# Scoring VectorE's block ahead of the single block in an attention kernel on Trainium2

## The chip, the cores and the metric

The kernel runs on one NeuronCore of a Trainium2 chip. The metric is the device time of one execution in microseconds. TensorE (PE) multiplies matrices, ScalarE (ACT) evaluates functions such as the exponential, VectorE (DVE) and GpSimd (POOL) do elementwise work, and SyncE (SP) issues transfers. Each engine works through its own instruction list in order; semaphores tie the lists together.

## The reference

Two transformer layers of self-attention and a feed-forward part, on 2048 rows of 512 numbers in bfloat16, 32 heads of 16:

```python
def _A_ref(x, wqkv, wo):
    H = 32; Dh = D // H
    q, k, v = split(x @ wqkv)                 # by head
    scores = jnp.einsum("bhqd,bhkd->bhqk", q, k) * Dh ** -0.5
    p = softmax(scores, axis=-1)
    o = jnp.einsum("bhqk,bhkd->bhqd", p, v)
    return merge(o) @ wo

def _B_ref(x, w1, w2):                        # w1: 512 x 1792
    return silu(x @ w1) @ w2

x = A_x
x = x + _A_ref(_layernorm(x), A_wqkv, A_wo)
x = x + _B_ref(_layernorm(x), B_w1, B_w2)
x = x + _A_ref(_layernorm(x), A_wqkv, A_wo)
x = x + _B_ref(_layernorm(x), B_w1, B_w2)
return x
```

`split` and `merge` stand for the reshapes and transposes by head.

## The kernel before

**Blocks and steps.** The attention scores are cut into blocks: one head, 128 keys (one k tile, `kt`), 512 queries. Four heads that lie on four strips of 32 partitions (`j` = 0 to 3) make a group of four blocks; a step handles one group. The steps are one long list, over both layers, the query chunks `qc`, the head groups `g`, two parities `par` and the 16 k tiles: 1024 of them after the opening. In each step `score` issues one matmul per block, with 32 contraction rows, so that the four of a step sit on different row strips of TensorE's array.

**Who makes the exponentials.** Nearly every step has four blocks in three kinds of home:
- the *pair*: two blocks in a two-bank PSUM tile (tag `s2`, two such tiles in turn), for one ScalarE exponential over 1024 numbers per partition;
- the *single block*: one bank (tag `s1`, one buffer), for a ScalarE exponential over 512;
- *VectorE's block*, d: one bank (tag `sd`, one buffer, tile `d_ps`). `emit_d` scores it and VectorE turns it into the bits of a half-precision approximation of the exponential with one `tensor_scalar` into `d_y` (L1001). It belongs to the group that is four steps ahead. Whenever two d blocks are done, GpSimd makes two more terms from them (`d_z`, L1021).

Steps 5 to 12 have no d block of their own and two single blocks (`n1 == 2`, the second one in the bank `sd`). ScalarE does the exponential of the single block first, then that of the pair (both L1083). Every second step, `emit_pv` issues the products of the probabilities with the values (L876).

**The order of TensorE's list.** A loop in Python writes every engine's list by hand (`manual_schedule`), step by step: the pair, the single block, d, then copies of finished sums, the products with the values if it is their turn, the exponentials, and last background work. All engines are in order: a matmul that waits for its bank holds up all matmuls behind it.

**The planner.** Background work (projections, layer norm, the feed-forward part, the closing of finished head groups) is written as generators that give way at each `part(...)` with its price. `Model` keeps a clock for TensorE (`pe`), ScalarE (`act`) and VectorE (`dve`), and the times at which banks come free: `s1`, `s2`, `sd`. `Model.scores` and `Model.score_d` move these on for a step's scores. `Background.heads` offers the next pieces, and `Model.fits` admits one if it ends before ScalarE would run out of work, and if what it needs has landed by the clock of its engine:

```python
if landed > (self.pe if pe else self.dve):
    return False
```

Three of these background pieces are named later. `group_out` closes a head group: after a DMA transpose of its sums into `ot` it takes a reciprocal (L601, priced 0.25) and multiplies (L603, priced 0.43) into `attn`. `ffn` computes one tile of the hidden layer with four matmuls into a bank with one buffer (`h_ps`, L466), in two halves of two matmuls; ScalarE takes a tanh of it (L649), and VectorE's `silu_mul` (L652) then reads the bank for the last time. `ln_apply` (L402) normalises rows and sends them through a DMA transpose. Where a step has no background matmuls and no products, `fill` adds matmuls with zero weights if the planner sees room.

Of the kernel before, what the change touches and what calls it, by code (L numbers as in the profile page):

```python
# [109 lines left out]
class Model:  # L110
# [26 lines left out]
            self.pe += self.SWITCH  # L137
            self.mode = mode

    def scores(self, a, d):  # L140
        self.to("S")
        self.pe = max(self.pe, self.s2[0], self.s1, self.sd if a == 4 else 0.0)
        self.scored = self.pe + self.GROUP + self.TO_ACT
        if d and a == 3:
            self.score_d()
        self.pe += self.GROUP

# [71 lines left out]
def kernel(  # L219
# [13 lines left out]
    S, D = xf.shape  # L233
# [96 lines left out]
    for par in range(2):  # L330
        m = const.tile([P, 1], FP32, name=f"mask{par}")
# [517 lines left out]
    def score(blk, out):  # L849
        L, qc, pi, g, par, kt, j = blk  # L850
        r = slice(32 * j, 32 * j + 32)
        nc.tensor.matmul(  # L852
            out,
            lhsT=KT[L, kt // 4][r, g, (kt % 4) * P : (kt % 4 + 1) * P],
            rhs=QT[g][r, par, :],
            start=True,
            stop=True,
        )
# [134 lines left out]
    def emit_d(t, blk):  # L993

        s_ps = psum["s"].tile([P, 512], FP32, name="d_ps", tag="sd", bufs=1)
        score(blk, s_ps[:])
        if not pairs or len(pairs[-1]["ds"]) == 2:
            y = dpool.tile([P, 2, 512], U16, name="d_y", tag="y", bufs=Y_BUFS)
            pairs.append(dict(ds=[], y=y))
        pr = pairs[-1]  # L1000
        nc.vector.tensor_scalar(  # L1001
            out=pr["y"][:, len(pr["ds"]), :],
            in0=s_ps[:],
            scalar1=float(1024 * SCALE * math.log2(math.e)),
            scalar2=float(1024 * (15 - SHIFT)),
            op0=ALU.mult,
            op1=ALU.add,
        )
        d = dict(blk=blk, pair=len(pairs), left=NT)
        d["rhs"] = [(t + 1, 0, pr["y"][:, len(pr["ds"]), :].bitcast(FP16))]  # L1010
        pr["ds"].append(d)
        d_todo.append(d)
        if len(pr["ds"]) == 2 or blk == last_d:
            other_terms(t, pr)
# [31 lines left out]
    with tc.manual_schedule(  # L1046
        engines={ENG.PE, ENG.Activation, ENG.DVE, ENG.Pool, ENG.SP}
    ):
        with psum_whole("a"):
            w_ps = bank("warm")  # L1050
            for i in range(56):
                nc.tensor.matmul(w_ps[:, 0:P], lhsT=ident[:], rhs=ident[:], start=True, stop=True)
            new_v(0, 0)
            xnT[0, 0] = xslot(0, "xnT")
            ln = [run(ln_stats(0, (i, i + 1))) for i in (0, 2)]
            for i in (0, 2):
                mv, rstd = ln[i // 2]
                xns = [ln_apply(0, i + u, mv[:, u, :], rstd[:, u, :]) for u in range(2)]
                ln_transpose(i, xns, xnT[0, 0], nc.vector.tensor_copy if i else nc.scalar.copy)
            bg.done["ln", 0, 0] = 0.0  # L1060
            bg.add(("k", 0, 0, 0), proj_k(0, 0, 0))
            bg.add(("q", 0, 0, 0, 0), proj_q(0, 0, 0))
            bg.ensure(("q", 0, 0, 0, 0))
        stream_psum = ExitStack()
        stream_psum.enter_context(psum_stream())
        for g in range(1, NG):
            bg.add(("k", 0, 0, g), proj_k(0, 0, g))
            bg.add(("q", 0, 0, g, 0), proj_q(0, 0, g))
            if g == 1:
                bg.add(("v", 0, 0), proj_v(0, 0))  # L1070
        for c in range(1, NC):
            bg.add_side(None, ln_ahead(c))
            bg.add_side(("ln", 0, c), ln_attn(0, c))
            bg.add(("k", 0, c, 0), proj_k(0, c, 0))
            bg.add(("v", 0, c), proj_v(0, c))
            for g in range(1, NG):
                bg.add(("k", 0, c, g), proj_k(0, c, g))

        m = Model(DVE_SLACK, PE_MARGIN)
        bg.model = m  # L1080

        def exp(p_sb, s_ps):
            nc.scalar.activation(  # L1083
                p_sb,
                s_ps,
                ACT.Exp,
                bias=-SHIFT * math.log(2.0) + math.log(EXP_SUM),
                scale=float(SCALE),
            )

        def flat(x):
            return x.rearrange("p a b -> p (a b)")

        def score_pair():
            return psum["s"].tile([P, 2, 512], FP32, name="s_ps", tag="s2", bufs=2)

        p_pre = hpool.tile([P, FT, 512], BF16, name="p_pre", tag="hT")
        pre = [score_pair() for _ in range(2)]
        for j in range(4):
            score(steps[0][0][j], pre[j // 2][:, j % 2, :])  # L1100
        for i in range(2):
            exp(flat(p_pre[:, 2 * i : 2 * i + 2, :]), flat(pre[i][:]))
        p_tiles[0] = [p_pre[:, i, :] for i in range(4)]
        m.act = 2 * m.EXP2
        m.s2 = [m.EXP2, m.act]

        early[0] = m.early = True
        bg.ensure(("q", 0, 0, 1, 0))
        for t in range(1, len(steps)):
            a_blks, d_blks = steps[t]  # L1110
            for L, qc, pi, g, par, kt, j in a_blks + d_blks:
                bg.ensure(q_of[L, qc, pi, g, par])
                if qc == 0:
                    bg.ensure(("k", L, kt // 4, g))
            L, qc, pi, g, par, kt, j = a_blks[0]
            if kt == kts_of[L, qc, pi, g, par][0]:
                for Lq, c, gq, n in q_next.get((L, qc, pi, g, par), []):
                    bg.add(("q", Lq, c, gq, n), proj_q(Lq, c, gq), first=True)
            s2 = score_pair()[:]
            n1 = len(a_blks) - 2  # L1120
            s1 = [
                psum["s"].tile([P, 512], FP32, name="s1_ps", tag=tag, bufs=1)[:]
                for tag in ("s1", "sd")[0:n1]
            ]
            for i in range(2):
                score(a_blks[n1 + i], s2[:, i, :])
            for i in range(n1):
                score(a_blks[i], s1[i])
            if n1 == 1:
                for blk in d_blks:  # L1130
                    emit_d(t, blk)
            m.scores(len(a_blks), len(d_blks))
            while after:
                after.pop()()
                m.sums()
            if t in pv_steps:
                m.pv(emit_pv(t, pv_step(t)))
            if t < D_LEAD:
                p = p_pre[:, 3 * t + 1 : 3 * t + 4, :]
                parts = [p[:, 0:n1, :], p[:, n1 : n1 + 2, :]]  # L1140
            elif n1 == 1:
                p = ppool.tile([P, 3, 512], BF16, name="p_sb", tag="p")
                parts = [p[:, 0:1, :], p[:, 1:3, :]]
            else:
                parts = [
                    dpool.tile([P, 2, 512], U16, name="p_z", tag=f"z{k}")[:].bitcast(BF16)
                    for k in range(2)
                ]
            p_tiles[t] = [p[:, i, :] for p in parts for i in range(p.shape[1])]
            for i in range(n1):  # L1150
                exp(p_tiles[t][i], s1[i])
            exp(flat(parts[1]), flat(s2))
            m.exps(len(a_blks))
            if t <= 4:
                bg.ensure(("v", 0, 0, t - 1))
            if t == 5:
                early[0] = m.early = False
            busy = t in pv_steps
            late = L == 0 or qc == 0
            while True:  # L1160
                for item in bg.heads(t):
                    if bg.fits(item) and (late or not item[2].pe or item[2].sums or t not in pv_steps):
                        break
                else:
                    break
                busy = busy or item[2].pe > 0
                bg.advance(item)
            if n1 == 2 and d_blks:
                m.late_d()
                emit_d(t, d_blks[0])  # L1170
            if not busy and m.fill_fits(FILL):
                n = fill(FILL)
                if n:
                    m.pv(n)
        t = len(steps) + 1
        emit_pv(t, pv_step(t))
        after.pop()()
        s_ps = score_pair()
        warm(3, s_ps[:, 0, :])
        bg.model = None  # L1180
        while bg.head(t + 5) is not None:
            bg.advance(bg.head(t + 5))
        warm(4, s_ps[:, 1, :])
        stream_psum.close()
        with psum_whole("z"):
            tail(1, NC - 1)
# [27 lines left out]
```

The softmax here doesn't subtract the row's maximum and nothing guards it: scores larger than these inputs give would overflow.

## Time and profile before

| | us |
|---|---|
| time, median of 3 runs | 1567.71 |
| lowest and highest run | 1567.08, 1571.06 |
| the profiled execution | 1566.55 |
| span of the profile | 1564.6 |
| mean granted TensorE clock | 0.992 |

| engine | busy us | share of the span |
|---|---|---|
| PE, matmuls | 1467.7 | 94% |
| ACT | 1511.7 | 97% |
| POOL | 1114.0 | 71% |
| DVE | 1078.8 | 69% |

The profile is of one execution. A row of a group names its line, engine and operation, what it writes and reads, how often it ran, its busy time and mean duration in ns, and the idle time of the engine just ahead of it with what ended most of that idle time. The list of waits adds up who waited for whom: total us, number of times, longest one. The timeline lists instructions by start and duration in us; an "x3" merges neighbours of one kind, and the brackets hold the idle time ahead of an instruction and its releaser. A wait for several semaphores is put down to the one that came last. Matmul records overlap, so that a busy PE is not one at its peak.

### The profile page before, as it was taken

Reading aid. Unit: us, or ns where it says so; the run is one execution under the profiler, and the core shown is the slowest. Engines: PE = TensorE matmul, PEld = TensorE weight load, DVE = VectorE, ACT = ScalarE, POOL = GpSimd, SP = SyncE. Lnnn points to the kernel's source line nnn. Section 1 sums busy time; section 2 is a strip of 40 time slices with the busy share of each in tenths; the row PEclk is TensorE's granted clock in tenths of the full one; section 3 lists DMA queues with packets and bytes.
Section 4 is the critical chain, followed back from the end, with each engine's and each line's share of the span. In section 5 each row is a group of like instructions: output and inputs, shape, how many; then the busy total and the mean of one; then the engine's idle time right before and its main releaser. Section 6 shows DMA issues by size and latency. Waiting matters only on the chain.

```text
span 1564.6 us, 34115 instructions
## 1 busy us (share of the span) xinstructions
PE 1467.7 (94%) x13311; PEld 460.2 (29%) x13311; DVE 1078.8 (69%) x1719; ACT 1511.7 (97%) x2177; POOL 1114.0 (71%) x1172
## 2 busy tenths in 40 slices
PE   7999998899989999899998999998999899989998
PEld 3222332232222322222222323322332232222223
DVE  6877677667766777667776667676677666766644
ACT  6999999999999999999999999999999999999982
POOL 2888777677876788677876777776777677776750
PEclk9999999999999999999999999999999999999999
DMA  4110013111121102201021010121012110120102
GB/s 140 30 28 2 5 38 62 31 32 28 45 48 25 36 21 55 49 18 44 16 52 41 8 34 10 23 62 32 21 42 61 29 31 15 45 51 22 28 15 51
DMA packets 154193, 55.82 MB, mean 36 GB/s; under 512 B 134064, under 2 KB 153520, under 8 KB 154032
## 3 DMA queue, kind: packets, MB, share of 16 engines
q1 hardware_dynamic: 154032, 53.65, 14.1%
q8 instruction: 104, 1.70, 0.4%
q14 instruction: 57, 0.47, 0.1%
HBM read 28.57 MB, written 4.19 MB: 21 GB/s over the span
## 4 chain that ended last, share of the span: by engine, by line
ACT 82%; PE 9%; DVE 4%; issue 3%; DMA 1%; POOL 1%; SPq 0%; DVEq 0%
ACT p_sb L1083 79%; ACT t_sb L649 3%; PE o_ps L876 3%; PE s_ps L852 2%; DVE d_y L1001 1%; PE h_ps L466 1%; PE f_ps L770 1%; PE d_ps L852 1%; DVE st L392 1%; DVE attn L603 1%; DVE xn L402 1%; SPq L517 0%; PE q_ps L466 0%; PE k_ps L466 0%; ACT p_pre L1083 0%
## 5 line engine op out<-in xcount | busy, mean ns | idle before, releaser
L1083 ACT ACTIVATE p_sb<-s_ps 128x512 bf16<-128x512 f32 x2026 | 1467.0, 1102 | 7.3 <-PE d_ps L852 6.1
L1001 DVE TENSOR_SCALAR d_y<-d_ps 128x512 uint16<-128x512 f32 x1012 | 696.9, 689 | 404.1 <-PE d_ps L852 360.9
L852 PE MATMUL s_ps<-QT,KT 32*128 32x512 bf16 x3084 | 630.6, 383 | 59.4 <-ACT p_sb L1083 44.9
L852 PE MATMUL d_ps<-QT,KT 32*128 32x512 bf16 x1012 | 390.1, 385 | 8.4 <-DVE d_y L1001 5.2
L852 PEld LDWEIGHTS <-KT 32*128 32x128 bf16 x4096 | 187.0, 91 | 647.3 <-issue 595.2
L876 PE MATMUL o_ps<-p_sb,VA 128*32 128x512 bf16 x3039 | 312.4, 389 | 8.2 <-DVE oB L981 1.1
L876 PE MATMUL o_ps<-d_y,VA 128*32 128x512 f16 x1012 | 153.4, 380 | 0.0
L876 PEld LDWEIGHTS <-VA 128*32 128x32 bf16 x4096 | 86.7, 95 | 160.0 <-issue 122.2
L711 PE MATMUL f_ps<-w_sb,hT 128*128 128x512 bf16 x392 | 104.0, 382 | 0.0
L876 PEld LDWEIGHTS <-VB 128*32 128x32 f16 x2024 | 78.4, 98 | 55.6 <-issue 0.8
L876 PE MATMUL o_ps<-w_qkv,zero 128*32 128x512 bf16 x1344 | 93.1, 383 | 0.0
L649 ACT ACTIVATE t_sb<-h_ps 128x512 f32<-128x512 f32 x98 | 86.5, 882 | 0.0
L652 DVE SCALAR_TENSOR_TENSOR hT<-t_sb,h_ps 128x512 bf16<-128x512 f32 x98 | 67.3, 686 | 22.6 <-ACT t_sb L649 22.3
L603 DVE TENSOR_TENSOR attn<-ot,rec 128x256 bf16<-128x256 bf16 x45 | 49.6, 1102 | 1.5
L981 DVE CAST oT<-o_ps 128x512 bf16<-128x512 f32 x64 | 43.5, 680 | 7.7 <-PE o_ps L876 7.7
L402 DVE TENSOR_SCALAR xn<-x,mv,rstd 128x512 bf16<-128x512 bf16 x64 | 42.6, 679 | 3.3 <-POOL rstd L397 1.8
L392 DVE BATCH_NORM_STATS2 st<-x 128x6 f32<-128x512 bf16 x64 | 43.5, 680 | 1.8 <-DMA x<-in_A_x_dram 1.8
L711 PEld LDWEIGHTS <-hT 128*128 128x128 bf16 x392 | 29.2, 97 | 46.4 <-issue 25.0
L876 PEld LDWEIGHTS <-zero 128*32 128x32 bf16 x1344 | 25.5, 95 | 40.2 <-issue 28.0
L466 PE MATMUL k_ps<-xnT,w_qkv 128*128 128x512 bf16 x128 | 35.4, 390 | 1.0 <-DVE xnT L431 0.9
L466 PE MATMUL q_ps<-xnT,w_qkv 128*128 128x512 bf16 x136 | 35.7, 382 | 0.0
L466 PE MATMUL v_ps<-w_qkv,xnT 128*128 128x512 bf16 x128 | 34.7, 382 | 0.1
(2319 smaller groups left out, 2057.4 us busy)
## 6 DMA issues: line engine op xcount, KB each, us to landing
wo<-in_A_wo_dram SPq DMA_DIRECT2D x8, 512.0 KB, 3.7
QT<-q SPq DMA_DIRECT2D x240, 16.0 KB, 1.8
x<-in_A_x_dram SPq DMA_DIRECT2D x7, 512.0 KB, 4.3
out_dram<-x SPq DMA_DIRECT2D x16, 128.0 KB, 1.7
w_sb<-in_B_w_dram SPq DMA_DIRECT2D x1, 1792.0 KB, 14.0
w_qkv<-in_A_wqkv_dram SPq DMA_DIRECT2D x3, 512.0 KB, 7.4
ot<-oT SPq DMA_TRANSPOSE x45, 2.3
x<-in_A_x_dram SPq DMA_DIRECT2D x2, 256.0 KB, 2.9
```

The lines of the kernel that those rows point to most:

```text
L392: nc.vector.bn_stats(st[:], x_sb[c][:, i, :])
L402: nc.vector.tensor_scalar(out=xn[:], in0=x_sb[c][:, i, :], scalar1=mv[:, 0:1], scalar2=rstd, op0=ALU.subtract, op1=ALU.mult,)
L466: nc.tensor.matmul(ps.rearrange("p (t q) -> p t q", q=P) if len(r.shape) == 3 else ps, lhsT=lhs(ct), rhs=r, start=(ct == 0), stop=(ct == C ...
L603: nc.vector.tensor_tensor(out=attn[L, qc][:, :, P * g : P * (g + 1)].rearrange("p t (j s) -> p t j s", s=32)[:, :, :, 16 * par : 16 * par ...
L649: nc.scalar.activation(t_sb, h_ps, ACT.Tanh, scale=0.5)
L652: nc.vector.scalar_tensor_tensor(out=hT[:, ft, :], in0=t_sb, scalar=1.0, in1=h_ps, op0=ALU.add, op1=ALU.mult)
L711: nc.tensor.matmul(y_ps, lhsT=hT[:, ft, tq * P : (tq + 1) * P], rhs=w2_sb[:, ft, :], start=(ft == 0), stop=(ft == FT - 1),)
L852: nc.tensor.matmul(out, lhsT=KT[L, kt // 4][r, g, (kt % 4) * P : (kt % 4 + 1) * P], rhs=QT[g][r, par, :], start=True, stop=True,)
L876: nc.tensor.matmul(o_tiles[key][32 * j : 32 * j + 32, :], lhsT=lhsT, rhs=rhs, start=(o_count[key][j] == 0), stop=stop,)
L981: nc.vector.tensor_copy(out=o, in_=o_tiles[key][:])
L1001: nc.vector.tensor_scalar(out=pr["y"][:, len(pr["ds"]), :], in0=s_ps[:], scalar1=float(1024 * SCALE * math.log2(math.e)), scalar2=float(10 ...
L1083: nc.scalar.activation(p_sb, s_ps, ACT.Exp, bias=-SHIFT * math.log(2.0) + math.log(EXP_SUM), scale=float(SCALE),)
```

## The change

In steps with one single block, the score of VectorE's block is issued right behind the pair and ahead of the single block, if the planner's clock says that its bank is free by the time that the pair can be scored (`m.sd <= m.pe`). In all other steps the order stays as it was. The planner books the d score accordingly, so VectorE's clock is moved on from the pair's time and not from the single block's. The rest of the code is the same.

```diff
-    def scores(self, a, d):
+    def scores(self, a, d, d_first):
         self.to("S")
+        if d and d_first:
+            self.score_d()
         self.pe = max(self.pe, self.s2[0], self.s1, self.sd if a == 4 else 0.0)
         self.scored = self.pe + self.GROUP + self.TO_ACT
-        if d and a == 3:
+        if d and a == 3 and not d_first:
             self.score_d()
         self.pe += self.GROUP
...
             for i in range(2):
                 score(a_blks[n1 + i], s2[:, i, :])
+            m.to("S")
+            m.pe = max(m.pe, m.s2[0])
+            d_first = n1 == 1 and m.sd <= m.pe
+            if d_first:
+                for blk in d_blks:
+                    emit_d(t, blk)
             for i in range(n1):
                 score(a_blks[i], s1[i])
-            if n1 == 1:
+            if n1 == 1 and not d_first:
                 for blk in d_blks:
                     emit_d(t, blk)
-            m.scores(len(a_blks), len(d_blks))
+            m.scores(len(a_blks), len(d_blks), d_first)
```

The changed kernel's line numbers are two higher up to this place in the loop (L601 becomes L603, L603 becomes L605, L652 becomes L654, L1083 becomes L1085 and so on).

## The prediction

> **What bounds the kernel now.** I read the engine totals first, then the costliest groups kept apart by shape, then the list of waits, then the timeline at the places where ScalarE stood still.
>
> ```profile
> PE 1467.7 (94%) x13311; PEld 460.2 (29%) x13311; DVE 1078.8 (69%) x1719; ACT 1511.7 (97%) x2177; POOL 1114.0 (71%) x1172
> ...
> L1083 ACT ACTIVATE p_sb<-s_ps 128x1024 bf16<-128x1024 f32 x1013 | 1333.9, 1317 | 0.0
> L1083 ACT ACTIVATE p_sb<-s_ps 128x512 bf16<-128x512 f32 x1013 | 897.9, 886 | 7.3 <-PE d_ps L852 6.1 <-PE s_ps L852 0.9
> L1001 DVE TENSOR_SCALAR d_y<-d_ps 128x512 uint16<-128x512 f32 x1012 | 696.9, 689 | 404.1 <-PE d_ps L852 360.9 <-PE s_ps L852 1.6 <-POOL d_z_16215 L1021 1.3
> ...
> PE s_ps L852 <- ACT p_sb L1083: 44.9, 108, 0.5
> ...
> PE h_ps L466 <- DVE hT L652: 6.5, 6, 1.4
> PE d_ps L852 <- DVE d_y L1001: 5.2, 9, 1.5
> ```
>
> ScalarE is the bound, and nearly the only one. The durations 886 and 1317 ns overlap, so their sum is not the price of a step. From end to end in the trace the 512-wide exponential takes 0.490 us and the 1024-wide 0.917 us, so a step is 1.407 us. Between the first exponential (13.9 us) and the last (1520.5 us) lie 1024 steps x 1.407 = 1440.8, two opening pairs = 1.8, eight extra 512-wide exponentials of early steps = 3.9 and 98 tanh x 0.490 = 48.0; 12.0 of the 1506.5 us are left over. Listed one by one, with the first exponential's own late start, they are 12.9 us at 29 places where an ACTIVATE ends later than its rate allows. VectorE waits 360.9 us for d scores and is not a bound by itself. All that the change can give is in those 12.9 us; 7.1 of them lie in the first 91 us and 1.5 around 250 us, where the first steps and layer-norm pieces that wait for a transpose hold VectorE and so TensorE.
>
> The other losses have a pattern. Five of them (0.560, 0.474, 0.285, 0.662 and 0.915+0.503 us at 267, 455, 642, 1051 and 1205 us; 3.40 together) are five of the six waits of h_ps for hT above. One of them:
>
> ```profile
> 638.90 0.24 DVE L601 RECIPROCAL rec<-ot 128x16 f32<-128x16 bf16 x1
> ...
> 639.14 1.04 POOL L1021 TENSOR_SCALAR d_z_10729<-d_y 128x1024 uint16<-128x1024 uint16 x1 [1.15 <-DVE rec L601]
> 639.18 1.28 DVE L603 TENSOR_TENSOR attn<-ot,rec 128x256 bf16<-128x256 bf16 x1
> ...
> 640.38 0.67 DVE L652 SCALAR_TENSOR_TENSOR hT<-t_sb,h_ps 128x512 bf16<-128x512 f32 x1
> 640.98 0.68 DVE L1001 TENSOR_SCALAR d_y<-d_ps 128x512 uint16<-128x512 f32 x1
> 641.17 0.13 PEld L466 LDWEIGHTS <-w_10651 128*128 128x128 bf16 x2 [1.34 <-issue]
> 641.20 0.59 PE L466 MATMUL h_ps<-fT,w_10651 128*128 128x512 bf16 x2 [1.07 <-DVE hT L652]
> 641.72 0.10 PEld L852 LDWEIGHTS <-KT 32*128 32x128 bf16 x4 [0.42 <-issue]
> 641.72 0.39 PE L852 MATMUL s_ps<-QT,KT 32*128 32x512 bf16 x3
> ...
> 642.19 0.60 ACT L1083 ACTIVATE p_sb<-s_ps 128x512 bf16<-128x512 f32 x1 [0.18 <-PE d_ps L852]
> ```
>
> The attention product (L603) takes 1.28 us beside a GpSimd operation, and the planner priced it at 0.43. Queued behind it on VectorE is the SiLU product (L652), whose end frees the one h bank; the next h matmuls wait 1.07 us for it, behind them wait the scores, and ScalarE runs dry. In VectorE's order, "L601, L603, L652 between two d_y" occurs at exactly these five places.
>
> **What the Trainium skill says.** "TensorEngine Tiling (Array Packing)", Key Properties: tiles of the array work independently. The trace agrees: where nothing waits, d starts 3 to 7 ns after the single block. "SBUF — State Buffer", Who interferes with whom: a VectorE operation with two SBUF inputs and a reading GpSimd operation block one another, and the earlier issue decides. The trace agrees: L603 from ot takes 0.43 us at least and 1.28 at the median. "TensorE: Matmul & The Clock Gate", Part 1: a monitor with a free-running window of about 3.4 us halves TensorE's clock after too little work. The trace has such stretches, one from 1203.4 to 1206.8 us at 0.50, right on the fifth place. "Perfetto Trace Analysis", Per-instruction lifecycle: a ScalarE record runs to the write's acknowledgement, hence the overlap above.
>
> **The change, part by part.**
>
> *The swap.* The orders of the two programs show d ahead of the single block in 329 of 1008 steps. Nothing is added or dropped there: the same four score matmuls. In the old order, the planner's condition holds in 336 steps; for these I took four times from the trace: pair, single block, d, and end of the previous d_y (plus 40 ns). Medians: the bank is free 50 ns before the pair, the single block starts 111 ns after the pair (it waits for ScalarE), and d 117 ns after. So d will start about 113 ns earlier, VectorE too. In only 7 of the 336 is the bank late, by 8 to 27 ns and once 138, while the single block (s1) may start up to 0.41 us after the pair before ScalarE loses time (0.60 from the pair to the point where ScalarE needs a finished score, less 0.18 of hand-over, which reproduces the losses at the places below). Price on ScalarE's path: 0. What does it buy? VectorE's 113 ns in steps where ScalarE had scores waiting: 0 too, hidden under 1.407 us of exponentials. The single block, now last, ends where d ended, so what follows on TensorE's queue does not move.
>
> *The added wait.* s1 now queues behind d's wait for VectorE, and ScalarE behind s1. VectorE is later than planned after L603. In the new order 7 swapped steps (200, 328, 456, 736, 752, 840, 856) free their bank with a d_y that follows L601 and L603; before, none did. At those steps the old trace has the bank free 0.915 us after the pair. The new order runs four f matmuls ahead of the pair instead of two (pair 0.36 later), and the previous swap starts VectorE 0.11 earlier: d and s1 at 0.915 - 0.36 - 0.11 + 0.01 = 0.45 after the pair, against the limit of 0.41. Loss 0.04 us each, at most 0.15: 7 x 0.04 = 0.3 (bounds 0 to 1.0).
>
> *The planner's other choices.* The planner's VectorE clock now falls earlier, and that moves background work. It admits an operation only when its transpose has landed by that clock. At step 181 the clock goes from past the landing (265.24 against 265.06) to before it (264.86 against 265.05), so L601 and L603 come one slot later: from a slot where L603 found GpSimd halfway (0.44 us at 285.94) into one right after a pair of d_y completes, where GpSimd starts on that pair, and directly ahead of L652. In the new program the pattern L601, L603, L652 stands at 12 places: the old five and seven new ones (steps 183, 311, 439, 719, 823, 935, 951), each with h split in halves as at the old five.
>
> Price of a new place: the third old one (642 us) has d at the nominal distance from ScalarE's need (0.48 us), and lost 0.285. In the new order d starts 0.113 earlier there: 0.17. Seven: 1.2 us. The first, second and fourth old place (larger losses) had TensorE late from before, d not waiting behind s1, and gain nothing; the third gains 0.05, the fifth 0.1. The fifth lost 1.418 because the clock fell; less 0.285 this is 1.13 for a fall. One fall in five places: 7 x 0.2 x 1.13 = 1.6 us. This term is an estimate: bounds 0 and 7.9.
>
> *Removed.* In each of three layer-0 chunks the losses of 0.115 us at 364, 552 and 739 us come from two L402 and an L603 within three steps; the new order parts them: -0.35. Thirteen fewer fillers (12 matmuls each, zero weights): they ran only where TensorE had room, so 0; they can cost clock, which is within the bounds above. DMA queues: the same transfers; on SP's queue the weights' loads of the feed-forward parts with a new place and the stores after them move back by two or so steps, with their matmuls; the load that TensorE did wait for (0.3 us at 262 us) stands ahead of the first new place. POOL's order keeps its pairs; only what belongs to the moved pieces shifts. Tail: same instructions.
>
> Sum: 0 + 0.3 + 1.2 + 1.6 - 0.15 - 0.35 = +2.6 us on the profiled span of 1564.6. The profiled execution itself counts 1566.55 and the others 1567.08 to 1571.06; added to the median, 1567.71 + 2.6 = 1570.3.
>
> **The rivals.** About 0.3%, 4.7 us, is what a measurement of this kernel can tell from no change.
>
> Slower: the seven new places cost what the old ones did on the mean, 3.40/5 = 0.68 us: +4.8, less 0.35, plus 0.3: 1572.5. With the clock falling at every one, 7 x (0.17 + 1.13) = 9.1: about 1576.7. It decides from 0.68 us per place. For it: all five old places lost. Against: three of them were late for another cause, a transfer or earlier work.
>
> Faster: 113 ns of VectorE lead in a third of steps dissolves losses elsewhere. If all losses after 80 us but those of the pattern went (4.3 us) and the five old places lost 0.11 less each, without new ones, 4.8 us: 1562.9. For it: VectorE stands in the chain of most of these losses. Against: at 250 us the swap isn't chosen (steps 158 to 161), and the pattern grows.
>
> Nothing: the swap is chosen but the moved work costs no more than before: 1567.7. Were the condition never true, it would come to the same; the orders exclude that.
>
> **How the numbers follow.** My sum as the likeliest has 0.50, with its own range 1567 to 1572.5; no effect 0.15; slower rival 0.29; faster 0.06. The first two are within 0.3%, save for edges that cancel: same 0.65, slower 0.29, faster 0.06. The range leaves out half of the faster rival and the worst of the slower: 1565.0 to 1576.5.
>
> **What would show it.** In the changed kernel's lines (two higher): the waits of h_ps for hT rise from 6 to about 13; ACT's idle before the 512-wide exponential rises from 7.3 us by 1 to 5; d_y's wait for d_ps stays near 360; the 1317 ns and end-to-end rates stay. At steps 200, 328 and the other five, s1 follows a d that waited for d_y. Wrong: fewer h_ps waits, or ScalarE losses at swapped steps of more than 0.15 us.

## The result, and the profile after

The changed kernel takes 1580.73 us (median of 6 runs, 1577.92 to 1584.66) against 1567.39 us (6 runs, 1565.80 to 1571.06): over all runs a ratio of 1.0081, 95% interval 1.0062 to 1.0099. It is slower, by 13.3 us between the medians where 2.6 were forecast, and outside the forecast range of 1565.0 to 1576.5 us. The profiled execution spans 1575.8 us against 1564.6, and its mean granted TensorE clock is 0.985 against 0.992.

The first fence has the page's engine totals and groups of the changed kernel, the second its list of waits (us in total, times, longest).

```profile
PE 1463.6 (93%) x13155; PEld 433.0 (27%) x13155; DVE 1076.3 (68%) x1719; ACT 1513.9 (96%) x2177; POOL 1115.1 (71%) x1172
...
L1085 ACT ACTIVATE p_sb<-s_ps 128x512 bf16<-128x512 f32 x2026 | 1461.4, 1056 | 15.5 <-PE d_ps L854 8.9
L1003 DVE TENSOR_SCALAR d_y<-d_ps 128x512 uint16<-128x512 f32 x1012 | 697.5, 689 | 410.2 <-PE d_ps L854 369.4
```

```profile
PE h_ps L468 <- DVE hT L654: 13.2, 12, 1.7
PE d_ps L854 <- DVE d_y L1003: 10.3, 19, 1.5
ACT p_sb L1085 <- PE d_ps L854: 8.9, 16, 1.2
...
DVE xn L404 <- POOL rstd L399: 3.6, 6, 1.0
```

ScalarE's own pace is what it was: from end to end its exponentials take 0.490 and 0.917 us as before (the recorded mean of the wide one did not stay, as the prediction had it, but fell from 1317 to 1272 ns; its cause is open). Its idle time before the 512-wide exponential has gone from 7.3 to 15.5 us, where a rise of 1 to 5 was forecast. The waits of h_ps for hT have doubled in number (6 to 12; about 13 were forecast), and so have those of d_ps for d_y (5.2 to 10.3 us) and of the layer-norm product xn for rstd (1.8 to 3.6 us). The last exponential ends at 1531.5 us instead of 1520.5, and the sum of ScalarE's losses (every ACTIVATE that ends later than its rate allows) is 23.9 us at 55 places instead of 12.9 at 29: the losses are the whole 11.0 us.

I sorted the losses by the clock. A stretch of half clock lasts 3.4 us; a loss is counted to it if its ACTIVATE starts from 0.2 us before the stretch to 0.9 us after it.

| ScalarE's losses, us | before | after | after less before |
|---|---|---|---|
| first 100 us | 7.12 | 7.31 | +0.2 |
| later, in half-clock stretches | 1.79 (2 stretches) | 9.47 (9 stretches) | +7.7 |
| later, at full clock | 3.99 | 7.13 | +3.1 |

So there are two separate things to explain: seven more stretches of half clock, and 3.1 us at full clock. The number of stretches in one execution is partly a draw. E1 below has the time of the kernel before over 14 runs, and six such stretches between 100 and 1500 us in its profiled execution. E3, whose order is that of the kernel before up to step 229 (some 356 us), has one at 160 us, where the changed kernel has one and the profile of before has none; so its 0.7 us cannot be put down to the change.

One of the new places of L603, L605, L654, at step 183, as the timeline of the changed kernel shows it:

```profile
287.96 0.24 DVE L603 RECIPROCAL rec<-ot 128x16 f32<-128x16 bf16 x1
...
288.20 1.04 POOL L1023 TENSOR_SCALAR d_z_4729<-d_y 128x1024 uint16<-128x1024 uint16 x1 [1.12 <-DVE rec L603]
288.24 1.28 DVE L605 TENSOR_TENSOR attn<-ot,rec 128x256 bf16<-128x256 bf16 x1
...
289.44 0.67 DVE L654 SCALAR_TENSOR_TENSOR hT<-t_sb,h_ps 128x512 bf16<-128x512 f32 x1
290.04 0.68 DVE L1003 TENSOR_SCALAR d_y<-d_ps 128x512 uint16<-128x512 f32 x1
...
290.26 0.59 PE L468 MATMUL h_ps<-fT,w_4648 128*128 128x512 bf16 x2 [0.96 <-DVE hT L654]
```

It is the mechanism of the prediction, down to the 1.28 us beside GpSimd's d_z; ScalarE loses 0.173 us at 291.25. All seven lose 0.172 to 0.175 us. What the prediction did not have is this, in VectorE's timeline of the same kernel, before a loss of 0.463 us at 371.54:

```profile
365.40 0.68 DVE L1003 TENSOR_SCALAR d_y<-d_ps 128x512 uint16<-128x512 f32 x1
365.99 1.14 DVE L404 TENSOR_SCALAR xn<-x,mv,rstd 128x512 bf16<-128x512 bf16 x1
367.06 0.67 DVE L1003 TENSOR_SCALAR d_y<-d_ps 128x512 uint16<-128x512 f32 x1
367.65 1.71 DVE L404 TENSOR_SCALAR xn<-x,mv,rstd 128x512 bf16<-128x512 bf16 x2
369.28 0.67 DVE L1003 TENSOR_SCALAR d_y<-d_ps 128x512 uint16<-128x512 f32 x1
370.42 0.69 DVE L1003 TENSOR_SCALAR d_y<-d_ps 128x512 uint16<-128x512 f32 x1 [0.46 <-PE d_ps L854]
```

Three layer-norm products stand in two successive gaps between d_y. The same three stood in two such gaps in the kernel before:

```profile
356.12 0.62 DVE L402 TENSOR_SCALAR xn<-x,mv,rstd 128x512 bf16<-128x512 bf16 x1
356.85 0.69 DVE L1001 TENSOR_SCALAR d_y<-d_ps 128x512 uint16<-128x512 f32 x1
357.46 1.53 DVE L402 TENSOR_SCALAR xn<-x,mv,rstd 128x512 bf16<-128x512 bf16 x2
358.91 0.67 DVE L1001 TENSOR_SCALAR d_y<-d_ps 128x512 uint16<-128x512 f32 x1
```

There they took 0.62 and 1.53 us; now they take 1.14 and 1.71, 0.7 us more, because they meet GpSimd's work at another moment: the first starts 0.04 us after a d_z (365.95 us), where before it started when a d_z (355.55 to 356.59 us) was half done. In the changed kernel's trace the 21 such products that run beside no d_z take 0.38 to 0.44 us each, the other 43 up to 1.27, 0.95 at the median. "SBUF — State Buffer" of the Trainium skill, Who interferes with whom, lists tensor_scalar among the operations that can take the port pair which VectorE shares with GpSimd, if its operands meet certain conditions; these durations agree. The next d_y starts at 369.28, and no wait stands ahead of it: VectorE itself is late. TensorE's d behind it waits 0.72 us for it (370.01 us), and ScalarE's exponential and the following d_y (which waits 0.46 us) come late after that.

Two more waits of TensorE, both for a transfer, are new or longer. At 378 us four projection matmuls wait for the transpose of the layer norm's rows, with the scores queued behind them:

```profile
378.00 1.64 PE L468 MATMUL k_ps<-xnT,w_qkv 128*128 128x512 bf16 x4 [1.20 <-DMA xnT<-xn]
```

At 454.75 us four h matmuls wait 1.22 us for their weights (w_7392), and ScalarE loses 0.516 us at 455.82; the same wait in the kernel before is 0.19 us, at 449.51 (w_7400). The load itself is no slower, 2.4 us from issue to landing against 2.6, but SP issues it behind its q transfers, 1.2 us ahead of TensorE's need instead of 2.5.

### The profile page after: what moved, and what is told of

Same layout as the page of the kernel before. It is cut to its first block, busy times and chain, and to the rows that moved or that the text cites. A ratio compares the mean times of both kernels' runs of the same rounds, so it can differ in the third digit from the quotient of the medians.

```text
span 1575.8 us, 33791 instructions
## 1 busy us (share of the span) xinstructions
PE 1463.6 (93%) x13155; PEld 433.0 (27%) x13155; DVE 1076.3 (68%) x1719; ACT 1513.9 (96%) x2177; POOL 1115.1 (71%) x1172
## 4 chain that ended last, share of the span: by engine, by line
ACT 76%; PE 12%; DVE 5%; issue 2%; DMA 2%; POOL 2%; SPq 1%; DVEq 0%; POOLq 0%
ACT p_sb L1085 73%; PE o_ps L878 3%; PE s_ps L854 3%; ACT t_sb L651 2%; PE h_ps L468 2%; DVE d_y L1003 2%; SPq L519 1%; DVE attn L605 1%; PE d_ps L854 1%; PE f_ps L772 1%; DVE hT L654 1%; PE q_ps L468 1%; DVE xn L404 0%; PE k_ps L468 0%; DVE st L394 0%
## 5 line engine op out<-in xcount | busy, mean ns | idle before, releaser
L1085 ACT ACTIVATE p_sb<-s_ps 128x512 bf16<-128x512 f32 x2026 | 1461.4, 1056 | 15.5 <-PE d_ps L854 8.9
L1003 DVE TENSOR_SCALAR d_y<-d_ps 128x512 uint16<-128x512 f32 x1012 | 697.5, 689 | 410.2 <-PE d_ps L854 369.4
L854 PE MATMUL d_ps<-QT,KT 32*128 32x512 bf16 x1012 | 392.6, 388 | 12.6 <-DVE d_y L1003 10.3
L854 PEld LDWEIGHTS <-KT 32*128 32x128 bf16 x4096 | 161.9, 91 | 637.9 <-issue 588.5
L654 DVE SCALAR_TENSOR_TENSOR hT<-t_sb,h_ps 128x512 bf16<-128x512 f32 x98 | 67.2, 686 | 26.2 <-ACT t_sb L651 26.0
L878 PE MATMUL o_ps<-w_qkv,zero 128*32 128x512 bf16 x1188 | 83.6, 387 | 0.0
L651 ACT ACTIVATE t_sb<-h_ps 128x512 f32<-128x512 f32 x98 | 78.7, 803 | 0.4 <-PE h_ps L468 0.4
L605 DVE TENSOR_TENSOR attn<-ot,rec 128x256 bf16<-128x256 bf16 x45 | 48.9, 1086 | 1.5
```

The lines of the kernel that those rows point to most:

```text
L605: nc.vector.tensor_tensor(out=attn[L, qc][:, :, P * g : P * (g + 1)].rearrange("p t (j s) -> p t j s", s=32)[:, :, :, 16 * par : 16 * par ...
L651: nc.scalar.activation(t_sb, h_ps, ACT.Tanh, scale=0.5)
L654: nc.vector.scalar_tensor_tensor(out=hT[:, ft, :], in0=t_sb, scalar=1.0, in1=h_ps, op0=ALU.add, op1=ALU.mult)
L854: nc.tensor.matmul(out, lhsT=KT[L, kt // 4][r, g, (kt % 4) * P : (kt % 4 + 1) * P], rhs=QT[g][r, par, :], start=True, stop=True,)
L878: nc.tensor.matmul(o_tiles[key][32 * j : 32 * j + 32, :], lhsT=lhsT, rhs=rhs, start=(o_count[key][j] == 0), stop=stop,)
L1003: nc.vector.tensor_scalar(out=pr["y"][:, len(pr["ds"]), :], in0=s_ps[:], scalar1=float(1024 * SCALE * math.log2(math.e)), scalar2=float(10 ...
```

## The experiments

Each kernel ran beside the kernel before on the same chip; the ratios are to those runs. There is one table for all, because the clock has to be read beside the time. "Clock" is the mean over all runs of the kernel, not that of the one profiled execution. Within a kernel's runs the time falls as the clock rises, by 0.7 to 1.3 us for each 0.001 (0.77 over the 101 runs of the kernel before beside E1 to E11, 0.9 over the six of the changed one). The last column moves the median to the clock of those 101 runs, 0.9904, at 0.9 us for each 0.001; it is an estimate, good to 1 us, and to some 2 us where the clock is furthest off (E3). Those 101 runs have a median of 1568.9 us.

| kernel | median us | ratio, 95% interval | clock | us at 0.9904 |
|---|---|---|---|---|
| changed | 1580.73 | 1.0081 [1.0062, 1.0099] | 0.9827 | 1573.8 |
| E1 swap only | 1568.73 | 0.9997 [0.9987, 1.0007] | 0.9906 | 1568.9 |
| E2 plan only | 1582.30 | 1.0081 [1.0065, 1.0097] | 0.9830 | 1575.6 |
| E3 before, 23 fillers fewer | 1579.51 | 1.0066 [1.0052, 1.0081] | 0.9772 | 1567.6 |
| E4 landing eased | 1567.83 | 0.9997 [0.9987, 1.0007] | 0.9909 | 1568.2 |
| E5 changed, small fillers | 1577.04 | 1.0051 [1.0037, 1.0066] | 0.9898 | 1576.5 |
| E6 eased, small fillers | 1571.80 | 1.0019 [1.0012, 1.0026] | 0.9905 | 1571.9 |
| E7 eased, SiLU ahead | 1570.87 | 1.0010 [1.0002, 1.0018] | 0.9901 | 1570.6 |
| E8 changed, fillers back | 1588.49 | 1.0125 [1.0111, 1.0140] | 0.9825 | 1581.4 |
| E9 before, 9 fillers fewer | 1574.42 | 1.0039 [1.0025, 1.0053] | 0.9842 | 1568.8 |
| E10 layer-0 packages only | 1576.88 | 1.0041 [1.0027, 1.0055] | 0.9863 | 1573.2 |
| E11 later packages only | 1572.71 | 1.0022 [1.0013, 1.0030] | 0.9867 | 1569.4 |

My theory from the two traces was: the swap is harmless, the replanned background work costs the time. The rival: the swap itself costs it, because the single block and ScalarE now queue behind d.

**E1 and E2, each half alone.** E1 swaps the scores but lets the planner book them as before; VectorE's, ScalarE's, GpSimd's and SyncE's orders are then those of before. E2 books the swap but issues the old order.

```diff
-            m.scores(len(a_blks), len(d_blks), d_first)
+            m.scores(len(a_blks), len(d_blks), False)
```

and E2:

```diff
-            if d_first:
-                for blk in d_blks:
-                    emit_d(t, blk)
...
-            if n1 == 1 and not d_first:
+            if n1 == 1:
```

> The swap alone: d is issued ahead of the single block in the 336 steps where the old planner's clocks say that its bank is free, but the planner books d as before, so that the lists of VectorE, ScalarE, GpSimd and SyncE are those of the kernel before. Replanning theory (the loss of the changed kernel, about 13 us, comes from the moved background work): 1566 to 1569 us, like before, granted clock 0.990 or more, TensorE's waits of h_ps for hT stay at 6, ScalarE's idle time before the 512-wide exponential near 7 us. Swap theory (d between the pair and the single block itself costs, by bank waits or by a falling clock): 1575 us or more, clock 0.986 or less. Filler theory (the 13 missing fillers let the clock fall): like before, since it has all 112 fillers.

> The replanning alone: the planner books d ahead of the single block as in the changed kernel, so that the lists of VectorE, ScalarE, GpSimd and SyncE are the changed kernel's, but TensorE issues the single block ahead of d in every step, as before. Replanning theory: 1576 to 1583 us, clock 0.986 or less, 12 to 13 waits of h_ps for hT; the seven new places cost 0.28 us each instead of 0.17, since d starts 0.11 us later. Swap theory: 1568 to 1571 us, clock 0.990 or more. Filler theory: 1576 us or more, since 13 fillers are missing.

E1: 0.9997; E2: 1.0081, the ratio of the whole change. The rival falls. By itself the swap costs nothing and, in 336 steps, brings nothing that these runs can tell; the booking alone makes the loss. At the seven new places the swap does help a little, as E2's text forecast: the three of them that lie at full clock in E2's profile (484, 673 and 1239 us) lose 0.274 to 0.277 us there, against 0.172 to 0.175 with the swap, so some 0.7 us over the seven.

**E4, the one decision undone.** In the kernel before, the attention item at step 181 passes the landing test by 0.18 us of the planner's clock; with the swap booked it fails by 0.19 and waits a slot. E4 is the changed kernel with this one test, for attention items, 0.2 us less strict.

```diff
-        return self.model.fits(item[2], self.done[item[2].need])
+        early = 0.2 if item[0] == "out" else 0.0
+        return self.model.fits(item[2], self.done[item[2].need] - early)
```

> The changed kernel with one test eased: an attention product may be admitted 0.2 us before the planner's clock reaches the landing of its transpose. VectorE's list is then nearly that of the kernel before (19 moved entries), with the pattern reciprocal, product, SiLU product between two d_y at 5 places and not at 12, 112 fillers, and the swap in place. Replanning theory: 1565 to 1570 us, clock 0.990 or more, 5 or 6 waits of h_ps for hT. Swap theory: 1576 us or more, clock 0.986 or less. Filler theory: like before.

0.9997, and the swap is still in. So the loss comes from those deferred items and what they drag along. The profiles of E1 and E4 have no wait for transposed rows near 378 us, and 0.1 us for the weights near 455; E2's has 1.07 and 1.19 us.

**E3, what fillers are worth.** The changed order has no filler in 23 steps that had one (ten others gained one). E3 takes the kernel before and leaves these out (276 matmuls with zero weights), still booked, so that nothing else moves.

```diff
+    NO_FILL = (229, 231, 233, 261, 263, 281, 357, 359, 361, 389, 391, 409,
+               485, 487, 489, 517, 519, 549, 617, 765, 869, 989, 991)
...
-                n = fill(FILL)
+                n = FILL if t in NO_FILL else fill(FILL)
```

> The kernel before without the filler matmuls (zero weights) of the 23 steps in which the changed kernel has none, 276 matmuls, still booked by the planner, so that nothing else moves. The output is the same. Filler theory: 1573 us or more, clock 0.987 or less. Replanning and swap theory: 1566 to 1570 us, clock 0.990 or more.

1.0066 with a clock of 0.9772: leaving out work that computes nothing costs 0.66%, and at the common clock nothing is left of it (1567.6). **E9** leaves out only nine of them, three steps in each of three layer-0 chunks: `NO_FILL = (229, 231, 233, 357, 359, 361, 485, 487, 489)`.

> The kernel before without its fillers at nine of the 23 steps, those of the layer-0 chunks ahead of layer-norm pieces (229, 231, 233, 357, 359, 361, 485, 487, 489); 108 filler matmuls fewer. If what a filler keeps up is the clock at these stretches above all: 1574 to 1578 us, two or more half-clock stretches each around 361, 552 and 747 us. If each filler step counts alike, 9/23 of the 0.66% of the 23: 1571 to 1573 us. If fillers don't set the clock and the loss of the 23 came otherwise: 1566 to 1570 us.

1574.42, in the clock theory's band, and its profile shows the cause directly. Stretches of E9: from and to, length, busy time and count of PE, PEld, DVE, ACT and POOL, then the granted clock (DMA share and GB/s are last):

```profile
356.40:359.80 3.40, 2.63 (x22) 0.69 (x21) 3.17 (x5) 3.40 (x7) 3.16 (x4) 1.00 0.24 54
359.80:366.70 6.90, 6.61 (x49) 1.29 (x48) 4.06 (x6) 5.76 (x9) 4.49 (x5) 0.51 0.38 46
```

The same stretches of the kernel before:

```profile
356.40:359.80 3.40, 3.36 (x36) 0.92 (x33) 3.07 (x5) 3.40 (x6) 3.16 (x4) 1.00 0.24 56
359.80:366.70 6.90, 6.52 (x85) 1.83 (x84) 4.73 (x7) 6.89 (x11) 4.81 (x6) 1.00 0.20 42
```

Without its 12-matmul filler the first stretch has 22 matmuls instead of 36, TensorE is busy 2.63 of 3.40 us, and the clock is halved for the next two windows; ScalarE, busy for 6.89 us in the kernel before, is busy for 5.76. The same happens at 551.0 to 557.8 and 738.7 to 745.5 us, at the other two groups of three steps (the window ahead has TensorE busy 2.34 and 2.71 us, 3.02 at these times in the kernel before), and nowhere else between 100 and 1500 us but at one old place (267.7 us).

**E5, is it the clock in the changed kernel?** To the changed kernel I added 416 unbooked filler matmuls: four in each step from 149 on that holds half an h tile, twelve in those at a place of the pattern. **E6** does the same to E4.

```diff
             busy = t in pv_steps
+            if t in HALF:
+                fill(3 if t in SITES else 1)
```

> The changed kernel with 416 more zero-weight filler matmuls, which the planner does not book, so that no other engine's list moves: one group of four ahead of the background matmuls in each step from 149 on that has only half a tile of them, and three groups at the 12 places where the h matmuls wait for the SiLU product, where TensorE stands idle anyway. The output is the same. Clock theory (the moved work leaves TensorE with thinner stretches, and its clock falls there): 1570 to 1575 us, granted clock 0.988 or more, at most 5 stretches of half clock between 100 and 1500 us instead of 9. Wait theory (the new waits themselves carry the loss): 1578 us or more, since the fillers take none of them away.

> The version with the eased landing test, with fillers added by the same rule (60 half steps, three groups at its five places). The output is the same. Clock theory: the remaining falls of the clock between 100 and 1500 us go too, 0 or 1 left, granted clock 0.992 or more, 1564 to 1567 us, 1 to 3 us under the version without them. Wait theory: no gain, 1567 to 1570 us, or a loss where a filler makes the pair late.

E5 brought the clock back (0.9898, 4 stretches between 100 and 1500 us), but the time only to 1577.04, between the bands of its two theories. E6 suggests why: there the same rule costs 0.19% [0.12, 0.26]. In E6 itself the clock theory failed: the last stretches were to go and 1 to 3 us to be gained, but its clock (0.9905) is that of E4 (0.9909), its profile has three stretches where E4's has two, and it is slower. So the clock part of E5 holds, and its number was missed because the fillers' own cost had been left out, as far as E6 carries over: at the common clock E5 stands 2.7 us above the changed kernel, and E6 3.7 above E4.

**E8, are the missing fillers to blame?** After E3 the simplest story was that the changed kernel lacks 23 fillers. E8 puts them back in exactly these steps.

```diff
-            if not busy and m.fill_fits(FILL):
+            if t in BACK:
+                fill(FILL)
+            elif not busy and m.fill_fits(FILL):
```

> The changed kernel with 276 filler matmuls put back, not booked by the planner, at exactly the 23 steps that lost theirs; the four other engines' orders stay those of the changed kernel. If the missing fillers are the cause of the losses around 371, 564 and 753 us and of most half-clock stretches: 1571 to 1575 us, a ratio of 1.003 to 1.005, a profiled clock of .987 or more, at most 5 half-clock stretches between 100 and 1500 us, and the losses of 0.46, 1.3 and 0.46 us at those three places gone. If the losses come from the waits that the moved work makes, and the clock only follows: 1578 to 1583 us, the three losses still there.

1.0125: worse by another 0.44%, outside both expectations. The story falls. TensorE's timeline of E8 at the first of the steps:

```profile
357.18 1.02 PE L469 MATMUL q_ps<-xnT,w_qkv 128*128 128x512 bf16 x4
358.13 0.83 PE L879 MATMUL o_ps<-w_qkv,zero 128*32 128x512 bf16 x12
358.89 0.39 PE L855 MATMUL s_ps<-QT,KT 32*128 32x512 bf16 x2
```

This step now holds projection matmuls (q_ps), moved there by the planner; E8's trace has two or four matmuls of real background work in each of the 23 steps (q_ps in 17). The filler comes on top of 1.02 us of real work, the scores behind it come late, and ScalarE loses 0.43 us at 359.39 (and at 551.66 and 742.08). The stretches remain nine in number, at other places, and the mean clock (0.9825) stays that of the changed kernel. So the planner was right to drop these fillers; the windows that let the clock fall in the changed kernel must be others.

**E7, the five remaining places.** E4 with the queue's head offered ahead of the attention item, so that L652's operation goes ahead of the attention product.

```diff
         return [
-            self.outs[0] if self.outs else None,
             self.head(now),
+            self.outs[0] if self.outs else None,
```

> The version with the eased landing test, and the planner offers a step's background piece (the SiLU product among them) ahead of the attention product instead of behind it. At the five old places VectorE then does the SiLU product first. If the chain L603, SiLU product, h bank is the cause there: waits of h_ps for hT fall from 5 or 6 to at most 1, ScalarE's losses at these places (about 2 to 3.5 us together) go, 1564 to 1567 us. If not, or if the late product now holds up d_y and the next scores instead: 1567 to 1571 us.

The waits of h_ps for hT are down to one of 0.3 us, but the time is 1.0010 [1.0002, 1.0018]: 0.95, 1.41 and 1.48 us are now lost at 555, 558 and 747 us, the first two in a half-clock stretch. It gives no gain.

**E10 and E11, where it is lost.** Against E4, VectorE's order in the changed kernel differs in seven separate packages: three long ones in layer 0 (about 107 d_y each, with layer-norm products and projections) and four short ones later. Each holds one new place. E10 keeps the long three, E11 the short four, by easing the test only after or only before step 700.

```diff
-        early = 0.2 if item[0] == "out" else 0.0
+        early = 0.2 if item[0] == "out" and self.now > 700 else 0.0
```

> The changed kernel with the landing test eased by 0.2 us for the attention items after step 700 only: VectorE's order then differs from the eased kernel's in the three layer-0 packages alone (between its scoring operations 173 and 279, 301 and 407, 429 and 535), with three of the seven new places; the swap is in place. If the loss sits in what is moved there (ScalarE lost 8.8 us between 290 and 820 us in the changed kernel against 1.1 in the kernel before): 1574 to 1578 us, and losses again near 371, 380, 564 and 753 us. If the seven places were to blame alike, 3/7 of the 0.81%: 1572 to 1574 us. If it is half-clock stretches that fall anywhere: no fixed share, and stretches also after 820 us.

> The same with the test eased before step 700 only: VectorE's order differs from the eased kernel's in the four later packages alone (47 scoring operations' surroundings, from 709 to 983), with four of the seven new places and no moved layer-norm piece of layer 0. If the loss sits in the layer-0 packages: 1569 to 1571 us (ScalarE lost 5.1 us after 820 us in the changed kernel against 2.6). If the seven places were to blame alike, 4/7 of the 0.81%: 1574 to 1576 us.

E10 gives 1.0041, in its expected band of microseconds; E11 1.0022, between the two bands given for it. They add up to the change within the noise: +0.41% and +0.22% against +0.81% [0.62, 0.99]; clock -0.0041 and -0.0037 against -0.0077; at the common clock +4.3 and +0.5 us against +4.9. So, by the estimate, the clock's share comes from both groups alike, and the rest from layer 0. In E10's profile the layer-0 losses stand at full clock: 0.457, 0.493, 0.303, 0.293, 0.573, 0.301 and 0.455 us at 370, 378, 385, 442, 560, 631 and 749 us, 2.9 together, with one half-clock stretch (479.1 us) between 290 and 820. They are no consequence of the clock. The one at 378 us is again TensorE's wait for transposed rows (0.81 us here).

## Why the prediction was wrong

The terms of its sum, against the changed kernel's profile:

| term | predicted us | measured us |
|---|---|---|
| the swap | 0 | 0 (E1) |
| single block behind a late d, seven steps | +0.3 | +0.13 |
| seven new places | +1.2 | +1.2 |
| clock falls | +1.6 | +7.3 |
| old places, at full clock | -0.15 | -0.6 |
| wait for weights at 455 us | 0 | +0.5 |
| layer-norm stretches of layer 0 and at 826 us | -0.35 | +2.3 |
| opening and rest | 0 | +0.2 |
| sum | +2.6 | +11.0 |

The clock's 7.3 is the 7.7 of the table above less 0.35 for two new places that lie in a stretch. It is too high as a price of the clock: 0.7 us are the stretch at 160 us, and about 1.1 us are the order's, since E10 loses 0.493 and 0.573 us at full clock (378 and 560 us) where the changed kernel has the stretches at 378 and 563 us. The 2.3 is -0.35 for the losses at 364, 552 and 739 us, gone as predicted, +1.85 for six new ones at full clock (371, 388, 444, 635, 753 and 767 us) and +0.75 at 826 us, where 0.88 us are lost instead of 0.14. The old places' -0.6 is not a gain of 0.6: the second now lies in a half-clock stretch and is counted there (0.956 and 0.354 us at 460 and 462), the third loses 0.61 instead of 0.29, the fourth 0.19 instead of 0.66. The forecast priced each one, and no single price came out.

**Right.** The swap's 0. Step 200 has its bank free late and its single block 0.454 us after the pair, against 0.45 in the text; the seven steps lose 0.016 to 0.021 each instead of 0.04. The places: all seven named steps, 0.17 us each, and 12 waits of h_ps for hT where about 13 were forecast. VectorE's wait for d scores stayed (360.9 to 369.4 us). The slower rival's price of 0.68 us per place is refuted, although its direction was right. Neither of the two things that were to show the text wrong (fewer h_ps waits, over 0.15 us lost at a swapped step) came about: both watched the swap and the places, and the loss came from elsewhere in the plan.

**Wrong, first: "One fall in five places: 7 x 0.2 x 1.13 = 1.6 us".** The mechanism was named and its bound (7.9) holds the measured 7.3, but by luck, since the term was tied to the seven places and to a rate taken from the five old ones. At the seven places themselves it was not too small: only two of the nine stretches (1238 and 1426 us) lie on a new place, and they cost 0.26 and 0.54 us beyond the place's own 0.17, 0.8 together. What it left out is the clock everywhere else; of the other seven, two lie on old ones (460 and 1214 us), and the rest at layer-norm or projection work or where no place is (160, 378, 563, 976 and 1153 us). The second reckoning, from the runs, gives the same size: (0.9904 - 0.9827) x 0.9 us per 0.001 = 7.0 us. That the clock is a cause, and not just a sign of waiting, is shown for the kernel before by E3 and E9, where only work that nobody waits for is taken away, and supported for the changed one by E5, which restores the clock by adding such work and is 3.7 us faster for it, with the fillers' own cost still in.

**Wrong, second: "the new order parts them: -0.35".** It did part L402 and L603. But I had followed only that pattern. The three layer-norm products in two gaps kept their gaps and met GpSimd's d_z at a worse moment (0.463 us at 371 and 753 us); other products now wait for rstd (at 444, 635 and 826 us), and an attention product stands ahead of scores beside projections (388 and 767 us). E10 has these losses in layer 0 without half clock, so the term is the order's own.

**Wrong, third: "they ran only where TensorE had room, so 0".** For a filler this argument misses what it does: where there is room it takes no time, and yet its absence costs, 0.39% for nine steps in E9. As an explanation of this change it fails too, though: E8 shows that these very steps had been given work.

**Wrong, fourth: the transfers, "with their matmuls", at nothing.** The weights' loads did move back with their matmuls, but not by the same amount: the wait at 455 us goes with a loss of 0.5 us. This wait varies: 0.38 to 1.22 us in the five profiles with the new plan there (changed, E2, E5, E8, E10), 0.10 to 0.57 in six with the old one (before, E1, E3, E4, E9, E11); so the plan makes it longer on the whole, and the amount in one execution is partly chance. The wait for transposed rows at 378 us, which costs 0.49 us in E10 at full clock, stands in the changed kernel, E2 and E10 alone, not in E5 and E8, which have the new plan and more fillers.

**The range** left the worst case of the clock out as a small part of one rival, though the upper bounds of its terms, 1.0 + 1.2 + 7.9 = 10.1, come near the 11.0 us measured. The two largest unknowns were both on the slow side and had one cause, the replanning, so they came together. (A slip without consequence: the losses after 80 us outside the pattern, 4.3 us in the faster rival, add up to 4.1.)

**Open.** Which thin window causes each of the seven added stretches was not settled. In the changed kernel every stretch between 100 and 1500 us follows a window of 3.4 us in which TensorE was busy for 1.7 to 2.7 us, but some windows just as thin (at 265.6 us, busy 1.94, and at 668.4 us, 2.24) were not followed by one. Four of the six stretches in E10's profile stand where VectorE's order is that of E4 (268, 995, 1056 and 1210 us), so how the layer-0 packages lower the mean clock is open too. Nor was the split of the layer-0 losses between GpSimd's interference, rstd's lateness, late transposes and work ahead of scores tried. No version beat both kernels; E1 and E4 equal the kernel before.

## What to carry to other kernels

When a planner decides the order, a change of one booking is a change of everything booked after it: take the decision that flips (here 0.2 us at one test) and price every package that it moves, not only the pattern that you were looking for. Where the clock answers to TensorE's activity, price thin windows over the whole run, and read the mean clock over all runs beside the time; a filler is then part of the work. Undoing half of a change in the order and half in the booking (E1 and E2) told cause from bystander in two runs.

## What the runs showed of the hardware

- A full idle window is not needed for half clock. "TensorE: Matmul & The Clock Gate" of the Trainium skill, Part 1, gives half rate as the state after at least one idle window of about 3.4 us; in E9 a window with 22 matmuls and TensorE busy 2.63 of 3.40 us was followed by two at half clock, where 36 matmuls and 3.36 us kept it full. The measurement decides; no threshold is known, and busy time alone does not decide: in the changed kernel a window with 20 matmuls, busy 1.94 us (from 265.6 us), was not followed by half clock.
- Over whole runs the time goes with the clock at 0.7 to 1.3 us per 0.001, and E3 and E9, where only fillers were left out, give 0.8 and 0.9 by their medians, although TensorE is not the bound: ScalarE does the paying, since scores at half clock come late (in E9's stretch it is busy 5.76 us instead of 6.89).
- The same 12 zero matmuls are worth 0.7 us a step where they keep a window busy (E9: 6.1 us for nine) and cost 0.3 us a step where real work fills it (E8: 7.6 us at the common clock for 23).
- A layer-norm product on VectorE (128x512, bfloat16) took 0.38 to 0.44 us beside no GpSimd d_z and up to 1.27 us beside one (21 and 43 cases in the changed kernel's trace).
